# The low halves of the expert weights: four of sixteen moved from GpSimd to VectorE

## The chip, the cores and the metric

The kernel runs on one core of a Trainium2 chip. Each time is device microseconds of one execution; the page and the trace come from one profiled execution of the same program. The core's engines are TensorE (PE, matmuls), VectorE (DVE), ScalarE (ACT), GpSimd (POOL) and SyncE (SP, which only issues DMAs here). Each runs its own program in order, and they wait for one another through semaphores.

## What is computed

Three layers follow one another: banded attention, a dense feed-forward layer with SiLU, and a mixture of eight experts in which each token goes to one expert. The change is in the third; the reference for it, cut to what matters:

```python
logits = x @ w_gate                       # x: 1536 x 512
e_idx = np.argmax(logits, axis=1)
gate_w = softmax(logits)[np.arange(N), e_idx]
eom = 1.0 / (1.0 + np.exp(-(x @ w_output_gate)))
for e in range(8):
    mask = e_idx == e
    h = np.maximum(x[mask] @ w1[e], 0.0)  # w1[e]: 512 x 1024
    ye = h @ w2[e]                        # w2[e]: 1024 x 512
    out[mask] = gate_w[mask, None] * eom[mask, e, None] * ye
```

All data are float32.

## The kernel before, in words

**Splits.** TensorE's fast float32 format holds fewer bits than float32, so each operand of a matmul is kept as two tensors: a high half (a copy of the value in the short format) and a low half (value minus high half). Products of high with high, high with low and low with high are summed. For the weights of the experts that is `split_u` (lines 543 to 549 load and split): ScalarE copies the loaded tile `qr` (128 x 512) into the high half (L548), then VectorE or GpSimd subtracts it from `qr` into the low half (L549). The result is a tile `uq` (or `qb` for the first four of every second expert). The argument `pool` says which engine subtracts. An expert has sixteen such tiles: four for the first half of w1, four for the first half of w2, then the second halves.

**Order of the work.** The experts are processed one after another, sorted by their number of tokens, largest first; here they are called expert 0 to 7 in that order. An expert has eight steps f, one for each 128 columns of its hidden layer; in step f, `f1_mm` (L678, L679 or L684) multiplies the tokens with w1's columns into a PSUM bank `h`, `f1_ev` evicts it into `hh` (called `hl` in expert 7), and `f2_mm` (L706 to L713) multiplies the `hh` of two steps before with w2 into the accumulators `y`. The eviction goes to and fro: ScalarE copies a part (`hs`, L690), VectorE adds it (L691), ScalarE applies the ReLU (L693), VectorE makes its low half (L696). Four PSUM banks in turn take `h`, the transposed rows of the next expert (`xm`, evicted into `xwT` by ScalarE in L670 and VectorE in L671) and `yf`.

**Where the splits stand.** The steps of an expert also make the sixteen tiles of the next one: none in steps 0 and 1, three each in steps 2 to 5, two each in steps 6 and 7 (`ns`). The first split of a step is recorded inside the eviction, between the addition and the ReLU (`between`), the others behind the eviction. Expert 0's own tiles are made in the layer before, and expert 7 makes none, so there are 7 x 16 = 112 of these splits in the trace from 400 us on, of which GpSimd has those with number 1, 5, 9 and 13: the second of step 2, the third of step 3, the first of step 5, the second of step 6.

**Loads and scatters.** SP loads the tiles `qr` in the order of use into eight buffers; a load waits until the split that used its buffer eight tiles earlier has read it, on both engines. At the end of an expert, `f2_ev` has ScalarE scale the `y` banks into SBUF (L723), and `put` (L635) has GpSimd scatter their rows into the output with an indirect DMA. Experts 0, 1, 5, 6 and 7 have a folded last tile: ScalarE copies half of the bank into `yl` (L721), one step later a PE matmul brings it to the other partitions (`yf`, L727), and VectorE adds it (L728) before its scatter. GpSimd's queue in this stage thus holds four splits and two or three scatters per expert, in the order in which they are recorded. In step 1 of expert 7 fourteen small VectorE instructions (`flags`, L508 to L521) stand ahead of the eviction.

Of the kernel before, what the change touches and what calls it, by code (L numbers as in the profile page):

```python
# [23 lines left out]
def kernel(ctx, tc, qk, v, n_global, n_local, w_in, w_out, wg, w1, w2, out):  # L24
# [402 lines left out]
    def logits(n):  # L427
        if n%2==0: glp[n//2]=abank([P,2,48 if n//2 in PU else 16],"gl")
        x=xts.pop(n)
        if n//2 in PU:  # L430
            for i in range(3):
                for k in range(KC): T.matmul(glp[n//2][:,n%2],x[:,i,k,:],wgb[:,k].rearrange("p j e -> p (j e)"),start=(i==0 and k==0),stop=(i==2 and k==KC-1))
            return
        for k in range(KC): T.matmul(glp[n//2][:,n%2],x[:,k,:],wgs[:,k,:],start=(k==0),stop=(k==KC-1))
# [50 lines left out]
    def order(c):  # L485

        k,o,w=cntf[:,0:8],cntf[:,8:16],cntf[:,16:32]
        g=abank([P,64],"gl")
        T.matmul(g[:,0:8],ones,esum[:,NTT if c else NTT-2],start=True,stop=True)
        V.scalar_tensor_tensor(out=k,in0=g[:,0:8],scalar=8.0,in1=rev,op0=ALU.mult,op1=ALU.add)  # L490
        if c:
            V.scalar_tensor_tensor(out=o,in0=rev,scalar=first,in1=k,op0=ALU.is_equal,op1=ALU.mult)
            V.tensor_reduce(out=w[:,0:1],in_=o,axis=AX.X,op=ALU.max)
            V.scalar_tensor_tensor(out=k,in0=o,scalar=-2.0,in1=k,op0=ALU.mult,op1=ALU.add)
        V.max(o,k)
        if c: V.tensor_copy(w[:,1:8],o[:,0:7])
        n=7 if c else 1
        o=o[:,0:n]; i=ordi[:,c:c+n]
        V.tensor_scalar(out=o,in0=o,scalar1=-1.0,scalar2=None,op0=ALU.add)
        V.tensor_copy(i,o)  # L500
        V.tensor_scalar(out=i,in0=i,scalar1=7,scalar2=7,op0=ALU.bitwise_and,op1=ALU.bitwise_xor)
        if c==0:
            V.tensor_copy(first,i)
            V.tensor_scalar(out=first,in0=first,scalar1=-1.0,scalar2=8.0,op0=ALU.mult,op1=ALU.add)
# [24 lines left out]
    def moe2_open2():  # L529
        es_m.close()  # L530
        m2['b']=es_2.enter_context(tc.tile_pool(name="m2b",bufs=1,side="left"))
# [3 lines left out]
    def wtile(name):  # L535
        return wp.tile([P,2,512],F32R,tag="wi",name=name,bufs=NWI)
# [7 lines left out]
    def split_u(k,i,pool=None):  # L544
        r=uqr.pop((k,i))
        t=m2['a'].tile([P,2,512],F32R,tag="qb",name="qb",bufs=NQB) if k%8==0 else wtile("uq")
        uq[k,i]=t
        A.activation(out=t[:,0],in_=r,func=AF.Copy)  # L548
        (G if (i%2 if pool is None else pool) else V).tensor_tensor(out=t[:,1],in0=r,in1=t[:,0],op=ALU.subtract)  # L549
# [34 lines left out]
    def late_split():  # L584
        xr=xrp[NTT//2-1]
        for t in range(2): ea['l',t]=halves(xr[:,t,:512],(G,V)[t])
    def late1():

        ea['c']=[ps.tile([P,2,W1],F32,tag=f"s2{k}",name=f"ec{k}",bufs=1) for k in range(2)]
        for k in range(KC):  # L590
            o=ea['c'][k//2][:,k%2]
            for j in range(2):
                n=min(P,W1-j*P)
                for a in range(2): T.matmul(o[:,j*P:j*P+n],ea['g',j][:,a,k*P:(k+1)*P],ea['I'][:,:n],start=(k%2==0 and j==0 and a==0),stop=False)
# [4 lines left out]
    def late3():  # L599
        for k in range(KC):  # L600
            for t in range(2):
                for a in range(2): T.matmul(ea['c'][k//2][:,k%2],ea['l',t][:,a,k*P:(k+1)*P],ea['o',t],start=False,stop=(k%2==1 and t==1 and a==1))
        for k in range(2):
            x=wp.tile([P,2,2,W1],F32R,tag="wi",name="xw",bufs=NWI)
            for i in range(2): xwT[0,2*k+i]=x[:,i]
            A.activation(out=x[:,:,0],in_=ea['c'][k],func=AF.Copy)
            V.tensor_tensor(out=x[:,:,1],in0=ea['c'][k],in1=x[:,:,0],op=ALU.subtract)
    def early1(hf,part):
        if part==0: ea['t']=s1bank([P,512],"eh")
        t=ea['t']; x=ea['xT']  # L610
        for k in range(6*part,6*part+6):
            ww,xx=((0,0),(0,1),(1,0))[k//4]; kc=k%4
            T.matmul(t,x[:,xx,kc,:],uq[2*hf,kc][:,ww],start=(k==0),stop=(k==11))
        if part==0: return
        h=m2['a'].tile([P,512],F32,tag="eh",name="ehs",bufs=2); ea['h',hf]=h
        A.activation(out=h,in_=t,func=AF.Relu)
    def early2(hf):
        h=ea['h',hf]; m=abank([P,4,P],"em")
        for k in range(4): T.transpose(m[:,k,:],h[:,k*P:(k+1)*P],ident)
        g=wtile("eg").rearrange("p a (k t) -> p a k t",k=4); ea['g',hf]=g  # L620
        A.activation(out=g[:,0],in_=m,func=AF.Copy)
        V.tensor_tensor(out=g[:,1],in0=m,in1=g[:,0],op=ALU.subtract)
    def early3(hf,part):
        if hf==0 and part==0: ea['y']=ps.tile([P,512],F32,tag="pv",name="ey",bufs=1)
        o=ea['y']; g=ea['g',hf]
        for k in range(2*part,2*part+2):
            w=uq[2*hf+1,k]
            for a,m in ((0,0),(1,0),(0,1)):
                T.matmul(o,g[:,a,k,:],w[:,m],start=(hf==0 and k==0 and a==0 and m==0),stop=(hf==1 and k==3 and m==1))
    def early4():  # L630
        y=m2['a'].tile([P,512],F32,tag="eh",name="eyo",bufs=2)
        A.activation(out=y,in_=ea['y'],func=AF.Copy,scale=ea['x'][:,512:513])
        put(y,ea['x'][:,TOK:TOK+1].bitcast(I32),P)
# [15 lines left out]
    def load_x(p):  # L649
        small(p); e=ereg(p)  # L650
        for k,s,n in tiles(p):
            x=m2['b'].tile([P,XW],F32,tag="xw",name="xw",bufs=6); xwt[p,k]=x
            S.dma_start(x,XE[ds(e*CAP+s,P),:])
    def load_t(p):
        small(p); e=ereg(p); s,k=tiles(p)[0][1],len(tiles(p))
        x=m2['b'].tile([P,k,XW-FAC],F32,name="xtail"); xwt[p]=x
        S.dma_start(x,XE[ds(e*CAP+s,k*P),FAC:XW].rearrange("(a p) d -> p a d",p=P))
# [73 lines left out]
    def folds():  # L731
        while late: late.pop(0)()
    nq=[0,0]; NQR=8; NQB=4
# [11 lines left out]
    def moe2():  # L745
        late_split()
        early1(0,0)
        run_gates(2)
        early1(0,1)
        logits(NTT-2)  # L750
        early1(1,0)
        run_gates(1)
        late1()
        run_gates(1)
        early1(1,1)
        run_gates(1)
        early2(0)
        late3()
        order(1)
        moe2_open2()  # L760
        load_x(1); load_t(0)
        early3(0,0)
        early2(1)
        early3(0,1); early3(1,0)
        early3(1,1)
        early4()
        atags[0]=['s1','s1b','a','pv']
        LG=2
        steps=[(p,f) for p in range(NE) for f in range(8)]
        for g in range(len(steps)+LG):  # L770
            if g<len(steps):
                p,f=steps[g]
                def spl():
                    split_u(4*(p+1)+nq[1]//4,nq[1]%4,nq[1]%4==1); nq[1]+=1
                f1_mm(p,f)
                folds()
                if p+1<NE and f==0: nq[:]=[0,0]
                if g==len(steps)-7: flags()
                ns=(0,0,3,3,3,3,2,2)[f] if p+1<NE else 0
                f1_ev(p,f,spl if ns else lambda: None)  # L780
                if p+1<NE:
                    for _ in range(ns-1): spl()
                    while nq[0]<min(16,nq[1]+4*(f+1),nq[1]+NQR): load_u(4*(p+1)+nq[0]//4,nq[0]%4); nq[0]+=1
                    if p and f==0: load_x(p+1)
                    if p==0 and f==5:
                        for k,s,n in tiles(0): tail(0,k,xwt[0][:,k,0:1],xwt[0][:,k,1:2])
                    t=tiles(p+1)
                    px=PX
                    if px<=f<px+len(t): prep_x(p+1,t[f-px][0])
            if g>=LG:  # L790
                p2,f2=steps[g-LG]
                if p2<NE-1:
                    f2_mm(p2,f2)
                    if f2==7: f2_ev(p2)
                    continue
                big,last=tiles(p2)
                if f2==7: f2_mm(p2,0,[big])
                f2_mm(p2,f2,[last])
                if f2==7:
                    f2_ev(p2,[last])  # L800
                    for k in range(1,8):
                        f2_mm(p2,k,[big])
                        if k==2: folds()
                    f2_ev(p2,[big])
# [233 lines left out]
    with tc.manual_schedule():  # L1038
# [27 lines left out]
        def run_gates(k):  # L1066
            for _ in range(min(k,len(gq))): gq.pop(0)()
# [114 lines left out]
```

## Time and profile before

| | us |
|---|---|
| three runs: lowest, median, highest | 589.2, 590.11, 590.27 |
| the profiled execution | 588.92 |
| its span in the trace | 587.2 |
| stretch of the experts, in the span | from about 396 to the end |

The page gives busy time per engine, and counts neither waits nor the issue of DMAs as busy. A timeline row gives the start (from the span's start), the duration, the engine, the line and the operation; a bracket at its end is the idle time of that engine just ahead of it and what ended it. Where a row stands for several instructions (x2, x3), its duration reaches from the first's start to the last's end. PE's ends are modelled.

### The profile page before, as it was taken

The page shows a single profiled execution, that of the slowest core. Times are in us where ns is not written, and L with a number is a line of the kernel's source. Part 1 is how long each engine was busy: PE and PEld are TensorE (multiplying, and loading weights), DVE is VectorE, ACT ScalarE, POOL GpSimd, SP SyncE. Part 2 cuts the span into 40 slices and gives each one's busy share as a digit, 9 for nine tenths or more (in the row PEclk, how much of TensorE's full clock was granted, in tenths as well). Part 3 has the DMA queues.
Part 4 walks back from the last instruction along what each step waited for, and adds up shares of the span by engine and source line. Part 5 has one row for each costly group of instructions (what it writes and reads, how often), then busy time and mean ns, then how long its engine had stood idle before and what let it go on. Part 6 is the DMA issues. An engine that isn't in the chain of part 4 may idle for free.

```text
span 587.2 us, 11814 instructions
## 1 busy us (share of the span) xinstructions
PE 565.8 (96%) x3939; PEld 475.4 (81%) x3939; DVE 389.9 (66%) x1088; ACT 302.9 (52%) x809; POOL 173.3 (30%) x214
## 2 busy tenths in 40 slices
PE   8999999999999999999999999999999999999983
PEld 3567888888888888888899999887787888887862
DVE  6885799998365756674645247646664887987940
ACT  7796334343444446343622326626656667767631
POOL 2367344443132431223111010213231332433311
PEclk9999999999999999999999999999999999999988
DMA  6666467697447877774473349219674668658400
GB/s 215 228 209 198 183 183 232 219 300 257 162 122 161 198 151 163 147 194 129 109 164 125 90 122 354 102 48 333 218 225 144 207 206 282 230 201 284 133 20 22
DMA packets 87530, 106.74 MB, mean 182 GB/s; under 512 B 35980, under 2 KB 50316, under 8 KB 87460
## 3 DMA queue, kind: packets, MB, share of 16 engines
q1 hardware_dynamic: 84692, 98.98, 56.8%
q0 software_dynamic: 2192, 6.39, 3.1%
q8 instruction: 33, 0.54, 0.4%
q10 hardware_dynamic: 576, 0.52, 0.3%
q14 instruction: 37, 0.30, 0.2%
HBM read 87.14 MB, written 17.66 MB: 178 GB/s over the span
## 4 chain that ended last, share of the span: by engine, by line
PE 64%; issue 10%; DVE 9%; ACT 6%; DMA 6%; POOL 3%; SPq 1%; POOLq 0%; DVEq 0%; ACTq 0%
PE s L339 19%; PE s L359 6%; PE s L360 6%; PE s L361 6%; PE qkp L170 3%; PE h L678 3%; DMA qr<-in_w_dram 3%; PE y L711 2%; PE y L713 2%; PE y L712 2%; PE pv L245 2%; PE h L684 2%; PE tp L206 2%; ACT uq L548 2%; PE h L679 2%
## 5 line engine op out<-in xcount | busy, mean ns | idle before, releaser
L339 PEld LDWEIGHTS s<-xT,wi 128*128 128x128 f32 x1152 | 147.4, 190 | 12.0 <-DVE g L348 5.6
L339 PE MATMUL s<-xT,wi 128*128 128x256 f32 x1152 | 152.0, 284 | 1.3 <-DVE xn L233 0.9
L343 ACT ACTIVATE u<-s 128x256 f32<-128x256 f32 x96 | 35.5, 381 | 102.6 <-PE s L339 100.8
L344 DVE SCALAR_TENSOR_TENSOR s<-u,s 128x256 f32<-128x256 f32 x96 | 39.7, 426 | 72.4 <-ACT u L343 72.4
L549 DVE TENSOR_TENSOR uq<-qr,uq 128x512 fp32r<-128x512 f32 x87 | 76.8, 902 | 8.0 <-ACT uq L548 5.8
L359 PE MATMUL s<-woh,g 128*128 128x512 f32 x192 | 79.4, 413 | 0.0
L360 PE MATMUL s<-woh,g 128*128 128x512 f32 x192 | 75.6, 394 | 0.0
L548 ACT ACTIVATE uq<-qr 128x512 fp32r<-128x512 f32 x112 | 66.7, 626 | 4.8 <-DMA qr<-in_w_dram 4.8
L348 DVE TENSOR_TENSOR g<-s,g 128x256 fp32r<-128x256 f32 x96 | 39.3, 422 | 30.9 <-ACT g L347 28.4
L347 ACT ACTIVATE g<-s 128x256 fp32r<-128x256 f32 x96 | 35.6, 381 | 40.8 <-DVE s L344 40.6
L549 POOL TENSOR_TENSOR uq<-qr,uq 128x512 fp32r<-128x512 f32 x25 | 32.3, 1300 | 55.2 <-ACT uq L548 43.9
L190 ACT ACTIVATE t<-t,mx 128x256 f32<-128x256 f32 (+1 forms) x96 | 45.7, 479 | 0.5 <-DVE mx L179 0.5
L359 PEld LDWEIGHTS s<-woh,g 128*128 128x128 f32 x192 | 36.3, 189 | 8.0 <-ACT u L343 2.7
L360 PEld LDWEIGHTS s<-woh,g 128*128 128x128 f32 x192 | 36.3, 189 | 5.2 <-DVE g L348 0.2
L693 ACT ACTIVATE hh<-h 128x192 fp32r<-128x192 f32 (+5 forms) x56 | 19.7, 352 | 39.7 <-DVE h L691 29.1
L361 PE MATMUL s<-wolr,g 128*128 128x512 f32 x128 | 39.7, 391 | 0.0
L635 POOL DMA_INDIRECT out_dram<-y,ixt x17 | 17.7, 1043 | 73.9 <-ACT y L723 33.8
L711 PE MATMUL y<-uq,hh 128*128 128x512 f32 (+1 forms) x88 | 36.7, 417 | 0.0
L197 POOL TENSOR_TENSOR hl<-t,hl 128x512 f16<-128x512 f32 (+1 forms) x18 | 19.9, 1104 | 50.1 <-ACT xT L269 12.2
L712 PE MATMUL y<-uq,hh 128*128 128x512 f32 (+1 forms) x88 | 34.6, 393 | 0.0
L713 PE MATMUL y<-uq,hh 128*128 128x512 f32 (+1 forms) x88 | 34.6, 393 | 0.0
L678 PE MATMUL h<-xwT,uq 128*128 128x448 f32 (+5 forms) x144 | 33.3, 354 | 0.6 <-DVE hh L696 0.4
(269 smaller groups left out, 1074.3 us busy)
## 6 DMA issues: line engine op xcount, KB each, us to landing
qr<-in_w_dram SPq DMA_DIRECT2D x128, 256.0 KB, 4.7
wolr<-wlo_d SPq DMA_DIRECT2D x64, 256.0 KB, 3.7
wiraw<-in_w_in_dram SPq DMA_DIRECT2D x16, 512.0 KB, 5.9
wraw<-in_w_out_dram SPq DMA_DIRECT2D x13, 512.0 KB, 11.2
ring<-in_qk_dram SPq DMA_DIRECT2D x22, 256.0 KB, 6.0
xe<-xe SPq DMA_DIRECT2D x7, 792.0 KB
wlo_d<-wol SPq DMA_DIRECT2D x16, 256.0 KB, 2.2
xw<-xe SPq DMA_DIRECT2D x15, 264.0 KB, 5.0
```

Source lines behind the costliest of these rows:

```text
L190: A.activation(out=t[:,j,:ce],in_=t[:,j,:ce],func=AF.Exp,scale=-1.0 if 4*n<SB else 0.125,bias=mx[n][:,h:h+1],accum_out=ss[n][:,h:h+1])
L339: T.matmul(t,w[:,ww,kc,:],x[:,xx,kc,:],start=(k==0),stop=(k==11)); k+=1
L344: V.scalar_tensor_tensor(out=t,in0=u,scalar=1.0,in1=t,op0=ALU.add,op1=ALU.mult)
L359: T.matmul(o,g[u][:,0,sl],wh,start=(f==0),stop=False)
L360: T.matmul(o,g[u][:,1,sl],wh,start=False,stop=False)
L361: else: T.matmul(o,g[u][:,0,sl],wl,start=False,stop=(f==FB-1))
L548: A.activation(out=t[:,0],in_=r,func=AF.Copy)
L549: (G if (i%2 if pool is None else pool) else V).tensor_tensor(out=t[:,1],in0=r,in1=t[:,0],op=ALU.subtract)
L678: for kc in range(KC): T.matmul(t[:,:2*W],uq[4*p+2*(f//4),kc][:,0,s],xwT[p,kc][:,:,:W],start=(kc==0),stop=False)
L711: T.matmul(o,hi,w[:,0],start=(f==0),stop=False)
L712: T.matmul(o,g[:,z:z+n],w[:,0],start=False,stop=False)
L713: T.matmul(o,hi,w[:,1],start=False,stop=(f==7))
```

## The change

One argument of one call changes: which engine subtracts.

```diff
                 def spl():
-                    split_u(4*(p+1)+nq[1]//4,nq[1]%4,nq[1]%4==1); nq[1]+=1
+                    split_u(4*(p+1)+nq[1]//4,nq[1]%4,False); nq[1]+=1
```

PE's, ScalarE's and SP's programs keep their order; the 28 instructions leave GpSimd's program and enter VectorE's at the place where they were recorded. Three places show it.

GpSimd, the end of its program for the experts (`L549` are splits, `L635` scatters, `x` counts equal rows in a row), the difference with - for before and + for the change:

```order
-L635 DMA out_dram<-y,ixt 1536x512 x2
-L549 TENSOR_TENSOR qb<-qr,qb 128x512
-L549 TENSOR_TENSOR uq<-qr,uq 128x512 x3
-L635 DMA out_dram<-y,ixt 1536x512 x2
-L549 TENSOR_TENSOR uq<-qr,uq 128x512 x4
-L635 DMA out_dram<-y,ixt 1536x512 x4
+L635 DMA out_dram<-y,ixt 1536x512 x17
 L1133 TENSOR_LOAD flag
```

What was a mixture of splits and scatters is now seventeen scatters in a row.

VectorE in steps 3 and 4 of expert 6, from the addition of step 3 to the addition of step 4 (`h1` is the PSUM bank, `hs` ScalarE's copy, `uq` a split's tile). Before:

```order
L691 TENSOR_TENSOR h1_7265<-h1_7265,hs_7275 128x184
L549 TENSOR_TENSOR uq_7278<-qr_7170,uq_7278 128x512
L696 SCALAR_TENSOR_TENSOR hh_7274<-h1_7265,hh_7274 128x120
L696 SCALAR_TENSOR_TENSOR hh_7274<-h1_7265,hh_7274 128x64
L549 TENSOR_TENSOR uq_7284<-qr_7199,uq_7284 128x512
L691 TENSOR_TENSOR h1_7301<-h1_7301,hs_7311 128x184
```

Now:

```order
L691 TENSOR_TENSOR h1_7265<-h1_7265,hs_7275 128x184
L549 TENSOR_TENSOR uq_7278<-qr_7170,uq_7278 128x512
L696 SCALAR_TENSOR_TENSOR hh_7274<-h1_7265,hh_7274 128x120
L696 SCALAR_TENSOR_TENSOR hh_7274<-h1_7265,hh_7274 128x64
L549 TENSOR_TENSOR uq_7284<-qr_7199,uq_7284 128x512
L549 TENSOR_TENSOR uq_7287<-qr_7201,uq_7287 128x512
L691 TENSOR_TENSOR h1_7301<-h1_7301,hs_7311 128x184
```

A second split (of `qr_7201`) stands behind the one that ended step 3, in front of the addition of step 4.

VectorE in step 5 of expert 6, inside the eviction. Before:

```order
L691 TENSOR_TENSOR h1_7345<-h1_7345,hs_7355 128x184
L696 SCALAR_TENSOR_TENSOR hh_7354<-h1_7345,hh_7354 128x120
L696 SCALAR_TENSOR_TENSOR hh_7354<-h1_7345,hh_7354 128x64
L549 TENSOR_TENSOR uq_7364<-qr_7256,uq_7364 128x512
L549 TENSOR_TENSOR uq_7367<-qr_7290,uq_7367 128x512
```

Now:

```order
L691 TENSOR_TENSOR h1_7345<-h1_7345,hs_7355 128x184
L549 TENSOR_TENSOR uq_7358<-qr_7254,uq_7358 128x512
L696 SCALAR_TENSOR_TENSOR hh_7354<-h1_7345,hh_7354 128x120
L696 SCALAR_TENSOR_TENSOR hh_7354<-h1_7345,hh_7354 128x64
L549 TENSOR_TENSOR uq_7364<-qr_7256,uq_7364 128x512
L549 TENSOR_TENSOR uq_7367<-qr_7290,uq_7367 128x512
```

Here the moved split (of `qr_7254`) stands between the addition and the low halves of the same step.

## Rows read from the trace of the kernel before

**Rows 1.** The page, part 1: busy us, share of the span, instructions.
```profile
PE 565.8 (96%) x3939; PEld 475.4 (81%) x3939; DVE 389.9 (66%) x1088; ACT 302.9 (52%) x809; POOL 173.3 (30%) x214
```

**Rows 2.** Table of stretches: from:to, length, then busy us of each engine, clock, DMA.
```profile
470.00:493.00 23.00, 23.00 (x127) 19.82 (x126) 19.52 (x38) 15.63 (x38) 7.37 (x6) 1.00 0.75 242
...
537.00:558.00 21.00, 19.72 (x115) 16.78 (x114) 17.55 (x52) 14.78 (x37) 7.46 (x6) 1.00 0.48 158
```

**Rows 3.** Timeline of PE: start, us, engine, line, operation, count, [idle before <- what ended it].
```profile
408.90 0.93 PE L678 MATMUL h<-xw,uq 128*128 128x384 f32 x4 [0.83 <-DVE hh L696]
...
415.41 1.78 PE L684 MATMUL h<-xwT,uq 128*128 128x272 f32 x12 [0.69 <-ACT xwT L670]
...
526.64 0.94 PE L678 MATMUL h<-xwT,uq 128*128 128x384 f32 x4 [0.39 <-DVE hh L696]
...
535.70 0.40 PE L708 MATMUL y<-uq,hh 128*128 128x512 f32 x1
...
538.27 0.44 PE L727 MATMUL yf<-yl,eI 64*64 64x512 f32 x1 [1.08 <-ACT yl L721]
...
560.66 0.44 PE L727 MATMUL yf<-yl,eI 64*64 64x512 f32 x1 [2.86 <-ACT yl L721]
```

**Rows 4.** Groups by line and form, 400 to 560: busy us, mean ns, idle before.
```profile
L549 DVE TENSOR_TENSOR uq<-qr,uq 128x512 fp32r<-128x512 f32 x75 | 68.6, 932 | 7.0 <-ACT uq L548 5.3
```

**Rows 5.** Timeline of DVE: splits alone and in a row, idle time.
```profile
430.82 1.89 DVE L549 TENSOR_TENSOR uq<-qr,uq 128x512 fp32r<-128x512 f32 x3
...
541.39 0.69 DVE L549 TENSOR_TENSOR uq<-qr,uq 128x512 fp32r<-128x512 f32 x1 [0.51 <-ACT uq L548]
...
549.77 0.42 DVE L696 SCALAR_TENSOR_TENSOR hh<-h,hh 128x120 fp32r<-128x120 f32 x2 [0.39 <-ACT hh L693]
```

**Rows 6.** Timeline of POOL: bursts of splits and a scatter.
```profile
458.42 3.80 POOL L549 TENSOR_TENSOR uq<-qr,uq 128x512 fp32r<-128x512 f32 x3
...
541.55 1.32 POOL L635 DMA_INDIRECT out_dram<-y,ixt  x1 [2.67 <-PE h L679]
542.89 2.54 POOL L549 TENSOR_TENSOR uq<-qr,uq 128x512 fp32r<-128x512 f32 x2
```

**Rows 7.** Timeline of DVE: splits that stood still.
```profile
403.58 1.25 DVE L549 TENSOR_TENSOR uq<-qr,uq 128x512 fp32r<-128x512 f32 x1 [0.94 <-ACT uq L548]
...
407.28 1.14 DVE L549 TENSOR_TENSOR uq<-qr,uq 128x512 fp32r<-128x512 f32 x1 [0.15 <-ACT uq L548]
...
458.46 4.92 DVE L549 TENSOR_TENSOR uq<-qr,uq 128x512 fp32r<-128x512 f32 x2
...
522.93 3.23 DVE L549 TENSOR_TENSOR uq<-qr,uq 128x512 fp32r<-128x512 f32 x1 [0.15 <-ACT uq L548]
...
543.26 2.73 DVE L549 TENSOR_TENSOR uq<-qr,uq 128x512 fp32r<-128x512 f32 x1
...
553.96 1.16 DVE L549 TENSOR_TENSOR uq<-qr,uq 128x512 fp32r<-128x512 f32 x1 [0.16 <-ACT uq L548]
```

**Rows 8.** Timeline of ACT: evictions ahead of PE's two longest waits.
```profile
536.92 0.68 ACT L723 ACTIVATE y<-y,sc 128x512 f32<-128x512 f32 x1
...
559.10 0.32 ACT L693 ACTIVATE hl<-h 128x176 fp32r<-128x176 f32 x1 [2.24 <-DVE h L691]
...
560.02 0.59 ACT L721 ACTIVATE yl<-y 64x512 fp32r<-64x512 f32 x1
```

**Rows 9.** Table of stretches, before and behind the longest wait.
```profile
540.00:556.00 16.00, 16.00 (x98) 14.11 (x97) 14.62 (x36) 11.65 (x29) 6.46 (x5) 1.00 0.46 142
...
562.00:563.00 1.00, 1.00 (x5) 1.00 (x4) 0.56 (x4) 0.32 (x1) 0.00 (x0) 0.50 0.78 213
```

**Rows 10.** Timeline of PE behind the longest wait: first matmuls of three steps.
```profile
561.91 1.38 PE L678 MATMUL h<-xwT,uq 128*128 128x352 f32 x4
...
564.73 0.81 PE L678 MATMUL h<-xwT,uq 128*128 128x352 f32 x4
...
566.29 0.81 PE L678 MATMUL h<-xwT,uq 128*128 128x352 f32 x4
```

## The prediction

> **What bounds the kernel now.** I read the page's first line first: TensorE (PE) is busy for 96% of the span, VectorE (DVE) for 66%, GpSimd (POOL) for 30% [rows 1]. So the question is not which engine has the most work but where PE stands still. The change touches only the last stage, the experts, from 396 us on, so I cut that stage by expert in the table of stretches [rows 2]. In most of it PE has no idle time at all; there, whatever VectorE and GpSimd do is hidden. In the stretch of expert 6 (537 to 558) PE is busy 19.72 of 21 us while VectorE is busy 17.55, 84%. (Experts are counted 0 to 7 in the order of work, steps f from 0 to 7; each expert's eight steps make the next one's sixteen splits.)
>
> Next, PE's own timeline: each row with a bracket is a wait, and the bracket names what ended it. Between 396 and 562 five of them are of a size to matter [rows 3]: 0.83+0.69+0.39+1.08+2.86 = 5.85 us. (Three more, below 0.4 each, I count at nothing.) Every one is ended by VectorE or by ScalarE (ACT), none by the transfer of a weight. That is about the most that this change can give back directly.
>
> Then I asked why VectorE is late there. A VectorE split takes 0.69 us alone, but 0.932 on average over the 75 of this stage [rows 4, 5]. The timelines of the two engines, side by side, show where the difference sits. At 458.42 GpSimd begins three splits in a row, 3.80 us; at 458.46 VectorE begins two of its own, which take 4.92 together instead of 1.29. The same happens at 543.26 (2.73 beside two) and at 522.93 (3.23), and in small, 1.1 to 1.3 each, at 403.58, 407.28 and 553.96 [rows 6, 7]. **A VectorE split that meets a GpSimd split stands still until GpSimd is done.** GpSimd's splits come in bursts because its queue is in order: a split that is ready stands behind a scatter that waits for its rows (at 541.55 one that waited 2.67 and then took 1.32, right ahead of the burst) [rows 6].
>
> **The change, part by part.** It removes 28 splits from GpSimd (four for each of seven experts), and adds the same 28 to VectorE's program at the places where they were recorded: two of four in steps 2 and 3 behind the step's evictions, one in step 5 between the two parts of an eviction, one in step 6. PE's, ACT's and SP's programs keep their order.
>
> *Added.* A VectorE split that follows another costs 0.60: three in a row take 1.89, one alone 0.69, so (1.89-0.69)/2 [rows 5]. 28 x 0.60 = 16.8 us more of VectorE work.
>
> *Removed.* The excess of the 75 splits is 75 x (0.932-0.69) = 18.2 us [rows 4, 5]. If the stalls all go, VectorE ends with about as much busy time as before (16.8-18.2 = -1.4 us in the whole stage). What changes is when: 3.6, 2.5 and 2.0 us lumps in steps 3 and 4, which put the chain of evictions late for the rest of the expert, become 0.6 us pieces, some of which fall into VectorE's idle time.
>
> [...] The rows show one VectorE split held over three GpSimd splits, 3.63 us in excess [rows 6, 7]. [...]
>
> *What reaches PE*, stretch by stretch:
>
> 1. Expert 0. PE waits 0.83 and 0.69 for VectorE and ACT [rows 3]. Until the second of them VectorE loses stalls of 0.56 (1.25-0.69 at 403.58) and 0.45 (at 407.28), 1.01 in all, and gains three splits, 1.80. Of these the idle 0.94 before 403.58 takes one whole (0.60), the 0.15 before 407.28 a part [rows 7], and the wait for ScalarE ahead of the eviction in step 5 (0.39 in the same place of expert 6, at 549.77 [rows 5]) a part of the third. 1.01-(1.80-0.60-0.15-0.39) = 0.35. I take 0.4.
> 2. Expert 5: the 0.39 at 526.64 is ended by an eviction that stood behind the stall of 522.93: 0.4.
> 3. The wait of 1.08 at 538.27. The matmuls that ACT evicts there were over at about 536.1 (the last is of 0.40 from 535.70 [rows 3]), but ACT began at 536.92 [rows 8], behind an eviction that waited for VectorE. 0.8 of that is VectorE's lateness in expert 5 (the stall of 3.23-0.69 = 2.54 alone [rows 7], against 2.4 of moved work that partly falls into idle time). The other 0.3 is ACT's own two copies and stays. 0.8.
> 4. The wait of 2.86 at 560.66. Followed back: ACT `yl` at 560.02, and ACT `hl` at 559.10, which waited 2.24 for VectorE [rows 8]; VectorE is busy from there back to 553.96 with few gaps, the small flag instructions among it. In expert 6 VectorE loses 2.04 (2.73-0.69) and 0.47 (1.16-0.69) of stalls and gains four splits: the first falls into 0.51 of idle before 541.39 and costs 0.1, the second 0.6, the third 0.6 less the wait of 0.39 at 549.77, the fourth 0.6 less the 0.16 before 553.96 [rows 5, 7]. 2.5-(0.1+0.6+0.2+0.45) = 1.15: 1.2. The wait would fall to some 1.7.
> 5. The clock. [...] A step's matmuls take 2.82 us there (561.91 to 564.73) and 1.56 in the next step (564.73 to 566.29); of the 1.25 from 560.66 to 561.91 the same share would be 1.25 x (1-1.56/2.82) = 0.56, and I take 0.4, as the fold itself may still have run at full clock [rows 3, 10]. That is 1.26+0.4 = 1.7 us. What does an idle of 1.7 do? The trace brackets it: after 1.08 at 538.27 the grant stayed at 1.00 (the row of 537 to 558 [rows 2]), after 2.86 it fell. Bounds 0 and 1.7; an idle of 1.7 lies nearer to 1.08, so I take the whole 1.7.
>
> Sum: 0.4+0.4+0.8+1.2+1.7 = 4.5 us. The profiled execution took 588.92 (span 587.2 and 1.7 around it), so 584.4 for one like it. It is 1.2 below the median of the runs shown, 590.11, hence **585.6** against that median.
>
> *What costs nothing and what hides it.* The scatters leave GpSimd earlier; PE does not wait for one. The weight loads on SP wait for the splits that free their buffers, GpSimd's among them; behind a VectorE split they are freed no later than behind a GpSimd split that takes about twice as long (3.80 for three, 1.89 on VectorE [rows 5, 6]). In experts 1 to 4 the moved work is hidden by PE's own matmuls (23.00 of 23 us in expert 3 [rows 2]); without that cover each expert would pay up to 4 x 0.60 = 2.4.
>
> **The rivals.**
>
> *A. The clock falls all the same.* Terms 1 to 4 come, 5 does not: 590.1-2.8 = 587.3. For it: nothing between 1.08 and 2.86 was measured.
>
> *B. VectorE becomes the bound: slower.* It is 84% busy in expert 6, and every eviction that PE's next bank needs passes through it. If the moved splits added 2.4 us per expert and the stalls did not come back (VectorE waiting for ScalarE's high halves instead, since each split needs one), the place is the wait at 560.66: 2.86+2.4, with the half clock kept, and some 0.5 in expert 5. 590.1+2.9 = 593.0. It decides from the point where VectorE's idle time in expert 6 (21-17.55 = 3.45) is not usable for more than 2.5 us of it. Against it: the stalls of 2.5 us there are plain in the rows and cannot outlive GpSimd's splits. [...]
>
> *C. The gain stays upstream.* The late evictions of experts 5 and 6 have another cause (ScalarE, which makes the high half for every split and stands in the same chain, or weights that land late), and only terms 1 and 2 come: 590.1-0.8 = 589.3, no measurable change.
>
> *D. More than forecast.* VectorE gets so far ahead that 560.66 keeps only ACT's copies, 0.4 of wait, and expert 0 loses both its waits: 4.5+(2.86-0.4-1.2)+(1.52-0.4) = 6.9, 583.2.
>
> That the change does not do what it says is ruled out by the order of the built program: GpSimd has no split left in this stage.
>
> **How the numbers follow.** Forecast 0.63; A 0.17; B 0.06; C 0.10; D 0.04. No change means within 0.2%, 1.2 us, about what a measurement of this kernel can tell (its three runs lie within 1.1). Faster: the forecast, A, D and a fifth of C, 0.86. Same: the rest of C, 0.08. Slower: 0.06. The range reaches from 583.2 (D) to 588.4 (A with half of its own 2.8 us lost); C and B are left out, under 2 in 10.
>
> **What would show it.** Right: the mean of VectorE's splits in this stage falls from 932 to about 690 ns, with no row above 1.3; VectorE's busy time hardly moves; the wait for `yl` near the end is below 2 us and the grant stays at 1.00 there; the wait at 538 falls to about 0.3. Wrong: VectorE rows of 1 us and more stay, or PE shows new waits for an eviction in steps 5 to 7 (rival B), or the wait near the end still exceeds 2.5 us (rival C), or it shrinks and the grant is 0.50 after it (rival A).

## The result, and the profile after

The changed kernel takes 583.82 us (median of 4 runs, 583.58 to 584.61) against 589.72 for the kernel before on the same chip (4 runs, 589.2 to 590.27): a ratio of 0.9902, interval 0.9885 to 0.9919. That is 5.9 us faster; where both were measured once more (e9 below) it was 5.3. The forecast was 585.6, the range 583.2 to 588.4. The profiled executions stand at 583.93 and 588.92, 4.99 apart, and it is this pair that the forecast's sum of 4.5 is held against.

The page after, part 1 (busy us, share of the span, instructions):

```profile
PE 563.6 (97%) x3939; PEld 474.7 (82%) x3939; DVE 388.0 (67%) x1116; ACT 304.9 (52%) x809; POOL 136.3 (23%) x186
```

VectorE has 28 instructions more and is busy 1.9 us less than before [rows 1]. GpSimd lost 28 instructions and 37 us. The groups of splits in the experts' stage, by line and form (busy us, mean ns, idle before), show why; GpSimd has no row of L549 left:

```profile
L549 DVE TENSOR_TENSOR uq<-qr,uq 128x512 fp32r<-128x512 f32 x100 | 66.5, 688 | 4.4 <-ACT uq L548 3.0
...
L549 DVE TENSOR_TENSOR qb<-qr,qb 128x512 fp32r<-128x512 f32 x12 | 7.9, 685 | 0.4 <-ACT qb L548 0.2
```

A hundred splits take 66.5 us; before, 75 of the same form took 68.6 [rows 4]. The mean is that of a split alone. Before, the longest took 4.32 us (all splits of this form in the program; shortest, median, longest in ns):

```profile
L549 DVE TENSOR_TENSOR uq<-qr,uq x87: 673/686/4322, 360.3 to 555.4; 128x512 fp32r<-128x512 f32 x87
```

After, the longest takes 0.96. The table of stretches after (from:to, length, busy us of PE, PEld, DVE, ACT, POOL, then clock, DMA share, GB/s):

```profile
470.00:493.00 23.00, 23.00 (x128) 19.83 (x127) 17.22 (x39) 15.87 (x36) 2.00 (x2) 1.00 0.71 232
537.00:558.00 21.00, 19.74 (x115) 17.06 (x115) 18.24 (x61) 15.46 (x39) 2.08 (x3) 1.00 0.36 120
558.00:562.00 4.00, 4.00 (x26) 3.57 (x26) 2.51 (x8) 1.57 (x7) 0.90 (x2) 1.00 0.24 64
```

The first two answer to [rows 2]: PE is full in expert 3 as before, and VectorE's share in 537 to 558 rose to 87%. The third stands where the grant was 0.50 [rows 9]; it is 1.00 now. PE's timeline after, the rows that answer to [rows 3] and [rows 10]:

```profile
409.04 0.94 PE L678 MATMUL h<-xw,uq 128*128 128x384 f32 x4 [1.02 <-DVE hh L696]
...
415.63 2.05 PE L684 MATMUL h<-xwT,uq 128*128 128x272 f32 x12 [0.68 <-ACT xwT L670]
...
536.63 0.44 PE L727 MATMUL yf<-yl,eI 64*64 64x512 f32 x1 [0.16 <-ACT yl L721]
...
557.41 0.44 PE L727 MATMUL yf<-yl,eI 64*64 64x512 f32 x1 [1.26 <-ACT yl L721]
558.35 0.81 PE L678 MATMUL h<-xwT,uq 128*128 128x352 f32 x4
559.91 0.81 PE L678 MATMUL h<-xwT,uq 128*128 128x352 f32 x4
```

The waits for `yl` fell from 1.08 to 0.16 and from 2.86 to 1.26, the 0.39 of expert 5 is gone, and the step behind the last fold takes 1.56 instead of 2.82. The two waits of expert 0 did not shrink. The same events of PE, after minus before, give an account of the whole difference, since PE's program is the same in both:

| from the event to the next | before | after | change | forecast |
|---|---|---|---|---|
| expert 0: its first step to the second of expert 1 | 395.12 to 418.18 | 395.10 to 418.68 | +0.52 | -0.4 |
| experts 1 to 4: on to a step of expert 5 | to 520.66 | to 520.61 | -0.55 | 0 |
| expert 5, first part: on to the step at [rows 3]'s 526.64 | to 526.64 | to 526.03 | -0.56 | -0.4 |
| expert 5, rest: on to the fold | to 538.27 | to 536.63 | -1.03 | -0.8 |
| expert 6: on to the last fold | to 560.66 | to 557.41 | -1.61 | -1.2 |
| on to the end of the span (most of it the clock) | to 587.2 | to 582.2 | -1.75 | -1.7 |

These sum to -4.98, with 0.02 more ahead of them. Of the last row, 1.57 stands where the forecast saw it: 0.31 from the fold to the next step and 1.26 in that step (2.82 to 1.56). The other 0.18 lies behind them and need not be the clock's: in the runs below whose steps behind the fold take 1.55 or 1.56 from the first on, the whole stretch from the fold to the end takes 24.50 to 25.11.

### The profile page after: what moved, and what is told of

It is laid out like the page before. It is cut to its first block, busy times and chain, and to the rows that moved or that the text cites. A ratio compares the mean times of both kernels' runs of the same rounds, so it can differ in the third digit from the quotient of the medians.

```text
span 582.2 us, 11790 instructions
## 1 busy us (share of the span) xinstructions
PE 563.6 (97%) x3939; PEld 474.7 (82%) x3939; DVE 388.0 (67%) x1116; ACT 304.9 (52%) x809; POOL 136.3 (23%) x186
## 4 chain that ended last, share of the span: by engine, by line
PE 69%; DVE 10%; issue 7%; ACT 6%; DMA 3%; POOL 3%; SPq 1%; POOLq 0%; DVEq 0%; ACTq 0%
PE s L339 18%; PE s L359 6%; PE s L360 6%; PE s L361 6%; PE h L678 5%; PE qkp L170 3%; PE y L711 3%; PE y L712 3%; PE y L713 3%; PE h L679 3%; PE pv L245 2%; PE h L684 2%; POOL wol L323 2%; PE tp L206 2%; DVE wt L296 2%
## 5 line engine op out<-in xcount | busy, mean ns | idle before, releaser
L549 DVE TENSOR_TENSOR uq<-qr,uq 128x512 fp32r<-128x512 f32 x112 | 74.6, 690 | 5.3 <-ACT uq L548 3.3
L635 POOL DMA_INDIRECT out_dram<-y,ixt x17 | 17.0, 1003 | 161.0 <-ACT y L723 129.0
L691 DVE TENSOR_TENSOR h<-h,hs 128x192 f32<-128x192 f32 (+5 forms) x56 | 20.9, 373 | 21.6 <-ACT hs L690 16.7
L170 PE MATMUL qkp<-ring 64*128 64x256 f32 (+1 forms) x192 | 32.7, 410 | 0.8 <-DVE mx L179 0.8
L678 PE MATMUL h<-xwT,uq 128*128 128x448 f32 (+5 forms) x144 | 32.5, 347 | 0.0
```

The source lines that it names most:

```text
L170: T.matmul(q[:,sl],w[:,z,1],w[:,z:z+1,0] if i==0 else w[:,0:3:2,0] if z==0 else w[:,z-1:z+1,0],start=True,stop=True)
L678: for kc in range(KC): T.matmul(t[:,:2*W],uq[4*p+2*(f//4),kc][:,0,s],xwT[p,kc][:,:,:W],start=(kc==0),stop=False)
```

## The experiments

The theory was that VectorE's splits stand still while GpSimd reads for its own, that this matters in experts 5 and 6, and that the last wait drags the clock with it. The rivals: the gain is spread over all experts; it comes from the low halves being made sooner, not from the stalls; and the last 1.7 is not the clock's. The kernel before took 589.39 (19 runs) on the chip of e1, e2, e3 and e5, and 590.41 (15 runs) on that of e4, e6, e8 and e9.

Executions differ by up to 2 us before the experts begin (last section), whatever the edit, so beside each median I compare the profiled experts' stage by itself. From the first matmul of L629 to the span's end it took 198.25 before (388.95 to 587.2) and 193.24 after (388.96 to 582.2). The columns "between folds" and "last fold to end" are differences of the starts of PE's two L727 rows and of the span's end.

| run | median | ratio, interval | stage | between folds | last wait | last fold to end |
|---|---|---|---|---|---|---|
| before | 589.72 | | 198.25 | 22.39 | 2.86 | 26.54 |
| after | 583.82 | 0.9902, 0.9885 to 0.9919 | 193.24 | 20.78 | 1.26 | 24.79 |
| e1, only experts 5, 6 | 584.58 | 0.9918, 0.99 to 0.9936 | 194.06 | 20.78 | 1.26 | 24.99 |
| e2, only experts 0 to 4 | 588.47 | 0.9988, 0.9971 to 1.0005 | 196.76 | 22.54 | 2.86 | 26.30 |
| e3, after, GpSimd reads | 591.79 | 1.0041, 1.0024 to 1.0059 | 200.78 | 23.51 | 3.04 | 26.34 |
| e4, after, GpSimd writes | 584.80 | 0.9906, 0.9881 to 0.9931 | 193.33 | 20.78 | 1.26 | 24.60 |
| e5, before, flags later | 586.59 | 0.9952, 0.9933 to 0.997 | 195.25 | 20.67 | 1.11 | 25.11 |
| e6, after, flags twice | 588.26 | 0.9964, 0.9945 to 0.9983 | 197.86 | 22.50 | 2.97 | 27.92 |
| e8, after, flags later | 582.94 | 0.9883, 0.9865 to 0.9902 | 191.15 | 19.67 | none | 24.50 |
| e9, after once more | 585.11 | 0.991, 0.9892 to 0.9928 | 193.34 | 20.80 | 1.26 | 24.73 |

**Which experts matter.** e1 moves only the splits that are made in the steps of experts 5 and 6, 8 of the 28 (the line of the kernel before, and what stands there instead):

```diff
-                    split_u(4*(p+1)+nq[1]//4,nq[1]%4,nq[1]%4==1); nq[1]+=1
+                    split_u(4*(p+1)+nq[1]//4,nq[1]%4,nq[1]%4==1 and p<5); nq[1]+=1
```

> Only the splits made in experts 5 and 6 move to VectorE (8 of 28); those made in experts 0 to 4 stay with GpSimd. Theory (VectorE splits stand still beside GpSimd splits, and this reaches TensorE only in experts 5 and 6 and behind them): nearly the whole gain, 583.4 to 584.8 us against 589.7 before. Rival (the gain is spread evenly over the seven experts, some 0.84 us each): 588.0 us.

e2 moves the other 20, those of experts 0 to 4:

```diff
-                    split_u(4*(p+1)+nq[1]//4,nq[1]%4,nq[1]%4==1); nq[1]+=1
+                    split_u(4*(p+1)+nq[1]//4,nq[1]%4,nq[1]%4==1 and p>=5); nq[1]+=1
```

> The other part alone: the splits made in experts 0 to 4 move (20 of 28), those made in experts 5 and 6 stay with GpSimd. Theory: next to nothing, 589.0 to 590.2 us against 589.7 before, the wait ahead of the last fold still near 2.9 us and the granted clock at 0.50 behind it. Rival (even spread): 585.5 us.

The eight give 4.8 us. The twenty give 0.9, with an interval that holds no change, and a median 0.5 below the range expected of them. The timeline of PE in e2 keeps the two waits for `yl`, and its table of stretches the half clock:

```profile
537.56 0.44 PE L727 MATMUL yf<-yl,eI 64*64 64x512 f32 x1 [1.00 <-ACT yl L721]
...
560.10 0.44 PE L727 MATMUL yf<-yl,eI 64*64 64x512 f32 x1 [2.86 <-ACT yl L721]
```
```profile
562.00:563.00 1.00, 1.00 (x7) 1.00 (x5) 0.41 (x2) 0.20 (x1) 0.00 (x0) 0.50 0.32 127
```

Yet more of the stalls went in e2 than in e1. The groups of L549 in the experts' stage, e2 first, then e1:

```profile
L549 DVE TENSOR_TENSOR uq<-qr,uq 128x512 fp32r<-128x512 f32 x93 | 67.1, 743 | 4.9 <-ACT uq L548 3.3
```
```profile
L549 DVE TENSOR_TENSOR uq<-qr,uq 128x512 fp32r<-128x512 f32 x82 | 67.0, 836 | 6.3 <-ACT uq L548 4.9
```

A mean of 743 ns and nearly no gain, a mean of 836 ns and most of it: how much VectorE loses says little; where it loses it says nearly all. A gain spread evenly over the experts falls. Yet e2's profiled stage is 1.5 us shorter than that of before, and 0.56 of this is in expert 5, whose splits GpSimd keeps: the wait of 0.39 [rows 3] is gone there.

```profile
526.11 0.88 PE L678 MATMUL h<-xwT,uq 128*128 128x384 f32 x4
```

GpSimd makes expert 5's splits in before and in e2, and PE waits 0.39 for an eviction there in the one and not in the other. That this hangs on which VectorE split the burst meets is the author's estimate and was not shown.

**Stalls, or low halves made too late?** Moving the splits ends the stalls and also has the moved low halves made faster. e3 keeps the changed kernel's splits and gives GpSimd, at the same 28 places, a subtraction that reads the new high half and whose result nobody reads:

```diff
-                    split_u(4*(p+1)+nq[1]//4,nq[1]%4,False); nq[1]+=1
+                    split_u(4*(p+1)+nq[1]//4,nq[1]%4,False)
+                    if nq[1]%4==1:
+                        h=uq[4*(p+1)+nq[1]//4,nq[1]%4][:,0].bitcast(F32)
+                        G.tensor_tensor(out=m2['a'].tile([P,512],F32,tag="dmy",name="dmy",bufs=1),in0=h,in1=h,op=ALU.subtract)
+                    nq[1]+=1
```

> The changed kernel, and GpSimd does at each of the 28 places a subtraction of the same size on the high half, into a tile that nobody reads: no result and no weight buffer waits for it. Theory (standing still beside GpSimd's reads is the cause): VectorE's splits average 0.9 us or more again, the wait ahead of the last fold is 2.5 us or more, the clock falls behind it, and with the moved work on top the time is 588 to 592 us. Rival (what hurt was that GpSimd's low halves came late and held buffers): 583.8 us, VectorE's splits at 0.69.

e4 has GpSimd fill a tile twice in the same places instead, which reads nothing. If its reads are the cause, VectorE's splits should stay at 0.69 us and the time at 584:

```diff
-                    split_u(4*(p+1)+nq[1]//4,nq[1]%4,False); nq[1]+=1
+                    split_u(4*(p+1)+nq[1]//4,nq[1]%4,False)
+                    if nq[1]%4==1:
+                        for _ in range(2): G.memset(m2['a'].tile([P,512],F32,tag="dmy",name="dmy",bufs=1),0.0)
+                    nq[1]+=1
```

> The changed kernel, and GpSimd does two fills of a 128 x 512 tile, which read nothing, at each of the 28 places. [...] Rival (any GpSimd work on that memory stops VectorE): splits of 0.8 us and more on average, 586 us or more.

The groups of the experts' stage in e3:

```profile
L549 DVE TENSOR_TENSOR uq<-qr,uq 128x512 fp32r<-128x512 f32 x97 | 80.2, 849 | 3.3 <-ACT uq L548 2.5
L777 POOL TENSOR_TENSOR dmy<-uq 128x512 f32<-128x512 f32 x24 | 31.6, 1315 | 52.8 <-ACT uq L548 52.4
```

and in e4:

```profile
L549 DVE TENSOR_TENSOR uq<-qr,uq 128x512 fp32r<-128x512 f32 x100 | 66.5, 687 | 4.5 <-ACT uq L548 3.2
L776 POOL MEMSET dmy<- 128x512 f32 x56 | 29.7, 530 | 2.8
```

GpSimd is busy about as long in both, but only its reads slow VectorE: 849 against 687 ns. With them the whole gain is lost and more (591.79, 1.0041 of the time before), and the last wait and the half clock are back:

```profile
563.76 0.44 PE L727 MATMUL yf<-yl,eI 64*64 64x512 f32 x1 [3.04 <-ACT yl L721]
```
```profile
566.00:568.00 2.00, 2.00 (x8) 1.70 (x7) 1.05 (x5) 0.64 (x2) 0.49 (x1) 0.50 0.04 12
```

Without them the time is that of the changed kernel (584.80 against e9's 585.11 on the same chip), though GpSimd's scatters stand behind the fills in its queue. Two stretches of the timelines show it row by row. In e3 a VectorE split meets two of GpSimd's (VectorE, then GpSimd):

```profile
459.15 2.03 DVE L549 TENSOR_TENSOR uq<-qr,uq 128x512 fp32r<-128x512 f32 x1
```
```profile
459.56 2.52 POOL L777 TENSOR_TENSOR dmy<-uq 128x512 f32<-128x512 f32 x2
```

In e4 eight fills run beside a row of splits and none is held:

```profile
544.55 4.65 POOL L776 MEMSET dmy<- 128x512 f32 x8
```
```profile
545.16 0.68 DVE L549 TENSOR_TENSOR uq<-qr,uq 128x512 fp32r<-128x512 f32 x1
...
546.16 1.30 DVE L549 TENSOR_TENSOR uq<-qr,uq 128x512 fp32r<-128x512 f32 x2
```

So the stalls are the cause, and not a low half that comes late from GpSimd: in e3 nobody reads what it makes. That e3 ends behind the kernel before fits its VectorE, which has 112 splits and the stalls; its page gives 403.8 us busy against 389.9 [rows 1].

**The last wait and the clock.** What is left of the last wait should be the fourteen flag instructions. The chain in the changed kernel, VectorE first and then ACT, has them between two evictions:

```profile
553.75 0.16 DVE L508 TENSOR_TENSOR cntf<-cntf,capk 128x8 f32<-128x8 f32 x1
...
555.39 0.17 DVE L521 CAST flag<-s_flag 128x10 int32<-128x10 f32 x1
555.47 0.34 DVE L691 TENSOR_TENSOR h<-h,hs 128x176 f32<-128x176 f32 x1
```
```profile
555.85 0.32 ACT L693 ACTIVATE hl<-h 128x176 fp32r<-128x176 f32 x1 [1.53 <-DVE h L691]
556.06 0.68 ACT L723 ACTIVATE y<-y,sc 120x512 f32<-120x512 f32 x1
556.76 0.59 ACT L721 ACTIVATE yl<-y 64x512 fp32r<-64x512 f32 x1
```

From 553.75 to 555.47 VectorE does nothing else, 1.72 us. e5 records them behind the last step, in the kernel before; e8 does the same in the changed kernel:

```diff
-                if g==len(steps)-7: flags()
...
+            if g==len(steps): flags()
```

> The kernel before, with the fourteen small flag instructions (1.7 us of VectorE) moved from step 1 of expert 7 to behind its last eviction. Theory (VectorE's lateness at that place sets the wait, and the wait drops the clock): the wait falls from 2.86 to about 1.2 us, the grant stays at 1.00, and the time is 589.7-1.7-1.7 = 586.3 us though GpSimd keeps its splits. Rival (the wait is set by GpSimd's bursts and the clock falls in any case): 588 to 589.7 us.

> The changed kernel with the flag instructions moved from step 1 of expert 7 to behind its last eviction. Theory: the wait ahead of the last fold falls from 1.26 to about 0.3 us (ScalarE's own two copies), 0.9 us less than the changed kernel: 582.9 us where that takes 583.8. Rival (another engine ends that wait next): no change against the changed kernel.

e6 doubles them in the changed kernel:

```diff
-                if g==len(steps)-7: flags()
+                if g==len(steps)-7: flags(); flags()
```

> The changed kernel with the fourteen flag instructions done twice in a row (1.7 us more of VectorE ahead of the eviction in step 1 of expert 7). Theory (that wait is VectorE's lateness, and its length decides whether the clock falls): the wait grows from 1.26 to about 3.0 us, the grant falls to 0.50 behind it, and the time is the changed kernel's 584 + 1.7 + 1.7 = 587.4 us. Rival (the clock hangs on something else than this wait): 585.7 us with the grant at 1.00.

e5 is a second way to shorten the last wait, with every stall left in place: 22.39 between the folds becomes 20.67, the grant stays at 1.00 in 561 to 563, and the last stretch falls from 26.54 to 25.11. So the two things, wait and clock, do not depend on who makes the low halves:

```profile
561.00:563.00 2.00, 2.00 (x13) 1.71 (x13) 1.40 (x4) 0.89 (x4) 0.06 (x1) 1.00 0.47 123
```

e6 goes the other way: no stall, but the wait grows by 1.71 and the clock falls. Its stretch behind the fold, and PE's steps there:

```profile
559.00:561.00 2.00, 2.00 (x6) 1.51 (x6) 1.26 (x4) 0.75 (x3) 0.23 (x1) 0.50 0.48 127
```
```profile
558.58 0.68 PE L727 MATMUL yf<-yl,eI 64*64 64x512 f32 x1 [2.97 <-ACT yl L721]
560.21 1.38 PE L678 MATMUL h<-xwT,uq 128*128 128x352 f32 x4
563.09 1.38 PE L678 MATMUL h<-xwT,uq 128*128 128x352 f32 x4
565.38 0.81 PE L678 MATMUL h<-xwT,uq 128*128 128x352 f32 x4
566.94 0.81 PE L678 MATMUL h<-xwT,uq 128*128 128x352 f32 x4
```

Steps of 2.88, 2.29 and then 1.56: here the clock cost 27.92-24.79 = 3.1 us, not 1.7. 1.7 us of small instructions on VectorE lengthened the profiled stage by 4.6. The clock was low from the fold on here: the fold took 0.68 us at 558.58, and 0.44 in the kernel before [rows 3], where the grant was 1.00 up to 561 and 0.50 from 561.5 to 564.5. In e6 it is 0.50 in 559 to 561 and in 562 to 563, and the first L678 row back at 0.81 is that of 565.38. By the medians the whole is 3.15 against e9, close to the 3.4 expected; e6's runs spread from 585.35 to 590.23, so other executions may have lost less to the clock.

e8 leaves no wait at the fold, where 0.3 was expected, and the grant is 1.00 from 540 to 570:

```profile
556.10 0.44 PE L727 MATMUL yf<-yl,eI 64*64 64x512 f32 x1
```
```profile
540.00:570.00 30.00, 29.85 (x171) 24.96 (x169) 21.39 (x75) 17.65 (x45) 2.94 (x4) 1.00 0.27 83
```

At 582.94 it beats both kernels, by a ratio of 0.9883 to the one before. That this is the number expected (582.9) is chance: it was to be 0.9 below the changed kernel, and is 2.2 below that kernel's time on the same chip (e9, 585.11). Against the changed kernel the profiled stage is 2.1 us shorter: 1.11 between the folds, 0.29 behind them, and the other 0.69 ahead of them, which the flags cannot explain: it lies in expert 0, whose part up to the second step of expert 1 took 22.83 instead of 23.58.

**Expert 0.** e9 is the changed kernel once more:

> The changed kernel itself, beside the others of this call on the same chip: 0.990 of the time before, 583.4 to 584.8 us, the wait ahead of the last fold near 1.3 us with the grant at 1.00. It also tells whether the first stretch (expert 0), where the forecast of 0.4 us less did not come, repeats: theory (the landing of the first weight load sets it, so the moved splits neither gain nor lose there): length from the first to the ninth step 20.0 to 20.6 us, longer where the load lands later.

It repeats the changed kernel's stage to 0.1 us, with the wait in expert 0 at 1.34. Its median, 585.11, is 0.3 above the range expected, and the eight steps of expert 0 took 20.66 where 20.0 to 20.6 was expected. What may set expert 0 is seen on ACT's timeline, at its first split of the next expert's weights; the row before and the row after:

```profile
400.95 0.63 ACT L548 ACTIVATE uq<-qr 128x512 fp32r<-128x512 f32 x1 [1.68 <-DMA qr<-in_w_dram]
```
```profile
401.48 0.63 ACT L548 ACTIVATE uq<-qr 128x512 fp32r<-128x512 f32 x1 [2.24 <-DMA qr<-in_w_dram]
```

The tile landed late in both, 5.83 and 6.38 us after the expert's first step. Over all runs the landing differs from 5.83 to 6.69 whoever makes the splits. The eight steps took 20.29 to 20.78 where GpSimd keeps expert 0's splits (before, e5, e1), and 19.80 to 20.74 where VectorE has them and GpSimd does not read (after, e2, e4, e6, e8, e9). The shortest three, 19.80, 19.92 and 20.31, are those with the tile at 6.04 to 6.17; the others have it at 6.38 to 6.60. So with an early tile the moved splits come out level with GpSimd's or up to 0.5 shorter, and with a late one level; these are ten profiles set side by side, and no run changes the landing alone.

## Why the prediction was right, and where not

The time, the mechanism and the sum (4.5 forecast, 5.0 measured in the profiled pair) held. That the sum came so near is partly luck: term 1 missed by 0.9, and 1.4 came beyond the forecast elsewhere. By its steps:

- **Removed and added work.** Right: 932 to 688 ns, VectorE busy -1.9 where -1.4 was forecast. "No row above 1.3" holds for single splits, whose longest took 0.96. e3 and e4 show that the stall is the cause and that GpSimd's reading makes it (849 ns beside its reads, 687 beside its fills).
- **Term 1, expert 0, is the step that failed.** It gave 0.4 and cost 0.52. The working added and took off stalls up to PE's second wait. It missed what stood behind the moved split at the expert's end. In the changed kernel VectorE's timeline has it ahead of the low half of the next expert's rows:

```profile
415.34 0.69 DVE L549 TENSOR_TENSOR uq<-qr,uq 128x512 fp32r<-128x512 f32 x1
415.95 0.42 DVE L671 TENSOR_TENSOR xwT<-xm,xwT 128x256 fp32r<-128x256 f32 x1
```

  That low half began at 415.39 before. PE's first step of expert 1 reads it and took 2.05 instead of 1.78 [rows 3]; 0.28 of the 0.52 is this. It is in every run: from that step to the next are 3.03 to 3.06 us where VectorE has expert 0's splits, and 2.76 or 2.77 in before, e1 and e5. The other 0.24 lies ahead of that step and goes with the landing of the first weight tile, 0.55 later in the profile after. The working had no load in it, though the 0.94 of idle ahead of a split [rows 7] said that VectorE was waiting there. That the landing is the cause is read from the profiles above and not shown by an experiment.
- **Experts 1 to 4 "cost nothing".** They gave 0.55, of it 0.53 in expert 2, between PE's steps at 464.04 and 469.97 (5.93 us; 5.40 after, 464.51 to 469.91). That is right behind the longest stall, the 4.92 at 458.46 [rows 7]: there PE waited 0.18 at 467.22 for VectorE's L671, one of the waits below 0.4 that the working left out, and its L678 took 1.16 at 464.04 and 1.08 at 467.22, where it takes 1.06 and 0.98 after. The cover was read from expert 3, where PE is busy for 23.00 of 23 us; in expert 2 (446 to 470) it was busy for 23.82 of 24.
- **Terms 2 and 3** had the right mechanism and were too small: 0.56 for 0.4, and 1.03 for 0.8. Term 2 is the one that e2 gains without moving expert 5's splits. The 0.3 that was to stay of the wait at 538 is 0.16.
- **Term 4** was too small, 1.61 for 1.2: the splits put on cost less than reckoned. The working let 1.05 us of them fall into VectorE's idle time; the timeline of before has 1.27 between 538.96 and 556 (0.51, 0.39, 0.21 and 0.16), and that of after none. The rest of the difference is open. The wait that stays, 1.26, is not stall at all: e8 moves the flags away and none of it is left. The working had the flags in the chain, but not as the whole of the rest. In the kernel before it is the two together: e5 keeps the stalls, moves the flags and leaves 1.11.
- **Term 5** came as sized, 1.75 for 1.7; the grants that it goes by stand in [rows 9]. The choice between its bounds, by the nearer of 1.08 and 2.86, was not put to the test: the wait came out at 1.26, and in no run does PE have one between 1.48 and 2.86 in this stage, so what the 1.7 of the working would have done stays open. That the loss can also be 3.1, as in e6, was not in the bounds.
- **The range.** Its upper end is told as rival A with half of its 2.8 us lost. That is 590.1-1.4 = 588.7, not 588.4; the result lies inside either way.
- **Rivals.** A (the clock falls) and C (the gain stays upstream) fall by the grant of 1.00 and the waits. B, the slower one, is what e3 made: stalls and added work together, 591.79; without the stalls VectorE at 87% carried the four splits. D, with the wait down to ACT's copies, came by way of e8 only.

## What to carry to other kernels

Before work is shared with a second engine, look at whether the first engine's own instructions get longer beside it: 28 splits given away here saved VectorE 16.8 us by the prediction's estimate and cost it 18.2 in stalls (1.9 us in all by the two pages), and they came in lumps. Then find which few places turn lateness into a wait of the bound engine; 8 of the 28 instructions alone gave 4.8 us, all of them 5.9. And look at what else stands in the chain of the last large wait: fourteen tiny instructions (1.7 us) were the rest of it, and recording them a few steps later brought 582.94.

## What the runs showed of the hardware

- VectorE splits were held for longer than one GpSimd split, which takes 1.3 us. The one of 3.23 us at 522.93 [rows 7] was held for 2.54, over two GpSimd splits in a row, and the longest, 4.32, for 3.6, over the three of 3.80 at 458.42 [rows 6]:

```profile
523.06 1.31 POOL L549 TENSOR_TENSOR qb<-qr,qb 128x512 fp32r<-128x512 f32 x1
524.33 1.28 POOL L549 TENSOR_TENSOR uq<-qr,uq 128x512 fp32r<-128x512 f32 x1
```

  By the starts in the profile it had begun before the first of these, as had the one of 2.03 in e3 (459.15 against 459.56), and both were held. Beside GpSimd's fills in e4 a split took 687 ns, as alone.
- Behind an idle of PE of 1.26 us in the changed kernel the grant was 1.00 (558 to 562), and so it was behind 1.34 in e9 (411 to 414) and in e3 (541 to 543). Behind the longest of this kind, 1.48 in expert 0 of e3, the step's first matmuls took 0.95, and 0.94 behind the 1.02 in the changed kernel:

```profile
410.31 0.95 PE L678 MATMUL h<-xw,uq 128*128 128x384 f32 x4 [1.48 <-DVE hh L696]
```

  Each idle of 2.86 to 3.04 (before, e2, e3, e6) was followed by a grant of 0.50, at a cost of about 1.5 to 1.75 us in before, e2 and e3, and of 3.1 in e6's profiled run, all against the changed kernel's last stretch.
- Executions of one program differ before the experts begin. A PE row of the same eight matmuls, in the changed kernel and in e9, the same program:

```profile
5.24 0.71 PE L170 MATMUL qkp<-ring 64*128 64x128 f32 x8
```
```profile
5.29 1.23 PE L170 MATMUL qkp<-ring 64*128 64x128 f32 x8
```

  In e9 PE's matmuls stay that slow until about 10 us, at a grant of 1.00, which puts it 0.65 behind. Its stage of the experts begins at 390.66 instead of 388.96: 1.7 us that no edit made. What decides it is open, and so is what makes the first weight tile of expert 0 land anywhere between 5.83 and 6.69 us after the step.
